# A gated linear recurrence with a gated feed-forward layer: the table that orders all steps is replaced

## The chip, the cores and the metric

The kernel runs on one core of a Trainium2 chip. Five engines work side by side, each through its own queue in order: TensorE (PE; its weight loads are listed as PEld), Vector (DVE), ScalarE (ACT), POOL and SP. SP computes nothing here; it issues DMAs, and so does POOL for the weights and for small accumulating transfers. They wait for each other through semaphores. The metric is the time of one execution in device microseconds; the lower, the better. The measure before is the median of 8 runs.

## The reference

Two parts, the second applied to the output of the first. Batch 4, 8 heads, 768 positions, head width 48; the model width is 8 x 48 = 384, the feed-forward width 1536.

```python
mag = np.sqrt(a_re * a_re + a_im * a_im)
scale = np.minimum(mag, 0.999) / (mag + 1e-06)
a_re_n, a_im_n = (a_re * scale, a_im * scale)
for t in range(S):
    ar, ai = a_re_n[:, :, t, :, None], a_im_n[:, :, t, :, None]
    new_re = ar * S_re - ai * S_im
    new_im = ar * S_im + ai * S_re
    kv = np.einsum('bhd,bhe->bhde', k[:, :, t], v[:, :, t])
    S_re, S_im = (new_re + kv, new_im)
    y[:, :, t] = np.einsum('bhd,bhde->bhe', q[:, :, t], S_re)

x = y.transpose(0, 2, 1, 3).reshape(B * S, H * D)
gate = 1.0 / (1.0 + np.exp(-(x @ w_gate)))
val = x @ w_val
out = gate * val @ w_out
```

The inputs and the output are float32.

## The kernel before

**Slabs and groups.** The 3072 rows are 24 slabs of 128 positions, numbered m = 0 to 23: chunk c of the sequence and batch b give m = 4c + b. SIZES puts the slabs into eight groups of 2, 2, 4, 4, 4, 4, 2 and 2: group 0 holds m = 0 and 1, group 1 m = 2 and 3, group 2 m = 4 to 7.

**Steps.** Every piece of work is a *step* with a kind and a number, written here as kind(number). The kinds that matter, by slab unless said otherwise:

- Loads by SP, 192 KB each (line 556): lr and la (the two parts of a), lk, lq and lv. Stores and small transfers of SP: scr and rbe (decays through DRAM), xk and xq (transposes by DMA, from m = 13), st (output).
- Weights by POOL: wg, wv (line 541) and wo (line 548), three pieces each. Piece i of wg and wv holds the feed-forward blocks 4i to 4i + 3, piece i of wo the same blocks' rows.
- Preparation of a: sq (583 on Vector for m = 2 to 8, else 586 on ScalarE), add (592) and min (599); for a whole group lna, inv and lnm (ScalarE 607, 618, 613), then r for two slabs (624) and atan for the group (702). add, min, r and qke are Vector's in group 0 and POOL's in all others.
- Prefix sums on TensorE: cl (633) of the logarithms and ct (722) of the angles, both in f32 with two instructions each. ee (640, 642) are two exponentials of cl. From chunk 1 on, hop (714, POOL) adds the last row of the chunk before to the angles by an accumulating DMA ahead of ct.
- r16 (728, Vector) rounds the turns, nid (735, TensorE) subtracts them, cr (745, ScalarE) keeps the last row for hop, ab (756, Vector) and cs (767 to 770, ScalarE) give cosine and sine.
- qke (695) multiplies q and k by the exponentials, ks and qs (780, Vector) by cosine and sine. v16 (688, POOL) casts v.
- tp (818, 819) transposes q and k on TensorE and qkT (825, Vector) copies them out, in two halves for each slab up to m = 12. sc (837, TensorE) are the scores of half the heads, mst (845, Vector) masks them.
- u and x16 (859, 868, POOL), kv (877, TensorE) and P (887, 890, Vector) carry the state from chunk to chunk. y (903, 905, TensorE) is the recurrence's output, y16 (522, Vector) its copy, xp (923, TensorE) transposes it, xt (929, Vector) copies it out as input of the feed-forward part.
- Feed-forward, for group g and block fb of 128 columns out of 12: pg(g,fb) and pv(g,fb) (942, TensorE, three matmuls each), tanh(g,fb) (952, ScalarE), p(g,fb) (958, Vector). For each slab, po(m,i) (978, TensorE) in three parts of four blocks, ot (522, Vector) and st.

**What sets the order.** The table TIMES holds one number for every step, and the program emits all steps sorted by it. Each engine's queue is this sorted list cut down to that engine. The numbers are sort keys: what counts is which is larger, and they cause no waiting. The waits come from data and buffers alone.

```python
order = sorted(self.steps, key=lambda k: (at[k], self.rank[k]))
...
for _ in range(WARM.get(key, 0)):
    nc.tensor.matmul(warm_of(tiles[st[2][0]]), zero, zero, start=True, stop=True)
st[0](tiles)
```

**Buffers.** The table SLOTS says which slot of a ring each new tile takes, in the order of the steps: two slots for a (group 2 takes the one of group 0, which ct(0) and ct(1) read last), five for q and k, three for v, four PSUM banks called gen (cl, ct, tp, sc, kv, y, xp) and four called moe (pg, pv, po). A step that takes a slot waits until its former holder's last reader is done.

**Dummies.** WARM puts matmuls of zeros, 128 x 128 (line 1012), in front of a step on TensorE. They write into the tile that the step is about to take, so they too wait until its slot is free.

**Tables of ScalarE.** lna and lnm need one function table, inv and ee one of two, atan one of two, tanh one of three, cs one of two. Where the sorted order goes from one kind to another that the loaded table doesn't hold, a table load is emitted (line 1006).

**The order at the start.** SP's loads are lr(0) la(1) lr(1) la(0) lr(2) la(2) lr(3) lk(1) la(3) lk(2) lv(4) lk(0) lq(1) lq(0) lv(1), and then, from the 16th on, lr(4) la(4) la(5) lr(7) lr(5) lk(3) lq(3) lq(2) lv(0) la(7) la(6) lr(6). lr(4) is the first into the slot that ct(0) and ct(1) free. POOL's steps are add(2) add(3) v16(4) min(2) **wg(1)** r(2) v16(1) add(4) **wv(1)** qke(3) add(5) qke(2) **wg(2)** min(4) v16(0) **wg(0)** add(7) add(6) **wv(2)** min(6) r(6) **wv(0)** r(4), the hops 4 to 7, qke(7) qke(4) **wo(1)** qke(5) add(8) v16(3) **wo(0)** v16(2) add(10) qke(6) **wo(2)**.

Of the kernel before, what the change touches and what calls it, by code (L numbers as in the profile page):

```python
# [36 lines left out]
        32.951, 14.583, 29.638],  # L37
    "wv": [
        41.185, 24.111, 37.481],
    "wo": [  # L40
        56.204, 51.226, 63.509],
    "lr": [
        0.04, 0.86, 3.16, 5.08, 13.925, 19.752, 28.021, 17.531, 29.623,
        62.128, 43.583, 64.048, 57.026, 74.047, 73.257, 65.008, 96.257,
        107.615, 110.045, 101.515, 137.663, 151.768, 166.927, 171.067],
    "la": [
        2.2, 0.45, 4.12, 7, 14.68, 15.64, 25.512, 24.552, 30.593, 69.119,
        51.877, 58.495, 61.138, 75.967, 72.847, 63.088, 97.077, 105.695,
        103.265, 102.675, 139.203, 141.828, 168.878, 168.468],
    "sq": [  # L50
        5.69, 4.73, 9.161, 10.49, 21.424, 23.242, 34.706, 33.84, 44.15,
        72.689, 57.636, 69.729, 66.044, 80.249, 76.577, 70.689, 104.472,
        112.973, 118.73, 115.322, 149.228, 158.967, 174.676, 175.97],
    "add": [
        6.559, 7.025, 10.178, 12.149, 22.441, 26.922, 36.527, 34.857, 53.807,
        73.594, 58.541, 70.634, 66.949, 89.758, 79.981, 72.602, 111.571,
        123.103, 119.884, 117.287, 150.133, 161.218, 175.581, 177.193],
    "min": [
        7.605, 13.68, 30.458, 38.521, 74.873, 71.699, 91.293, 87.116, 124.638,
        121.415, 162.282, 179.123],  # L60
    "lna": [
        6.558, 13.727, 35.687, 78.872, 83.739, 120.761, 160.998, 178.729],
    "lnm": [
        8.185, 15.332, 39.488, 82.363, 93.681, 125.605, 163.249, 180.206],
    "inv": [
        7.426, 14.595, 37.195, 80.986, 91.565, 126.982, 163.986, 180.943],
    "r": [
        8.295, 15.623, 42.005, 39.424, 82.531, 84.291, 93.956, 106.636,
        133.282, 137.885, 164.891, 181.848],
    "cl": [  # L70
        9.073, 9.719, 20.075, 17.308, 43.684, 45.402, 46.048, 42.48, 85.5,
        91.202, 87.197, 87.843, 109.442, 108.149, 111.386, 107.503, 148.529,
        150.473, 145.491, 154.559, 177.162, 179.303, 182.338, 182.984],
    "ee": [
        12.987, 12.247, 22.019, 22.759, 47.25, 48.311, 49.051, 46.51, 90.085,
        92.941, 89.345, 90.825, 111.417, 110.677, 112.233, 109.46, 152.06,
        151.32, 152.8, 155.406, 179.466, 188.022, 187.282, 188.762],
    "scr": [
        30.033, 30.313, 28.711, 28.431, 49.147, 48.867, 50.638, 56.303,
        91.661, 94.511, 90.731, 91.381, 115.548, 116.608, 114.858, 110.455,  # L80
        156.012, 152.178, 156.292, 156.982, 183.077, 198.269, 192.333, 192.613],
    "rbe": [
        47.412, 67.694, 70.599, 98.417, 129.307, 159.322, 213.64, 204.94],
    "lk": [
        9.88, 6.04, 7.96, 20.712, 35.106, 41.425, 53.205, 32.273, 78.847,
        81.727, 83.647, 77.887, 115.138, 96.667, 104.225, 133.664, 114.448,
        116.198, 156.572, 141.418, 176.447, 181.157, 169.288, 172.027],
    "lq": [
        11.8, 10.84, 22.632, 21.672, 38.894, 46.157, 55.893, 37.894, 79.807,
        92.351, 91.941, 82.687, 120.194, 101.105, 109.085, 134.074, 119.784,  # L90
        117.158, 157.262, 146.226, 177.407, 184.327, 178.947, 183.367],
    "lv": [
        23.592, 12.76, 50.228, 49.427, 8.92, 75.007, 80.767, 76.927, 92.761,
        84.607, 114.038, 111.965, 119.374, 136.703, 106.655, 128.527, 145.816,
        94.101, 111.005, 121.814, 191.923, 206.91, 205.76, 172.987],
    "v16": [
        31.509, 17.384, 57.244, 54.761, 13.104, 79.404, 86.539, 81.909,
        103.832, 104.408, 118.728, 120.839, 130.217, 145.197, 110.655,
        132.706, 169.908, 113.392, 127.88, 168.466, 198.411, 218.557, 220.232,
        183.609],  # L100
    "qke": [
        15.915, 14.389, 27.877, 25.162, 49.465, 52.046, 61.748, 47.704,
        95.717, 97.478, 99.239, 92.196, 128.457, 115.039, 135.043, 141.784,
        155.763, 152.242, 166.705, 157.524, 186.109, 196.651, 188.357, 193.916],
    "atan": [
        10.216, 19.618, 43.84, 86.41, 117.353, 147.043, 184.404, 190.796],
    "ct": [
        11.426, 13.076, 25.634, 21, 49.401, 50.047, 52.307, 54.263, 92.496,
        93.142, 95.408, 90.356, 130.362, 122.671, 135.255, 129.716, 155.205,
        163.471, 166.078, 164.117, 193.531, 197.936, 199.73, 198.917],  # L110
    "r16": [
        12.273, 13.923, 26.481, 25.575, 50.248, 50.894, 55.627, 62.519,
        93.343, 96.075, 99.028, 91.869, 133.139, 123.937, 138.869, 133.605,
        156.052, 164.944, 167.011, 169.332, 195.244, 199.482, 202.877, 203.943],
    "nid": [
        13.722, 14.523, 27.081, 26.727, 50.848, 51.817, 56.538, 64.118,
        95.245, 96.701, 104.303, 94.435, 135.093, 128.568, 141.444, 137.196,
        156.948, 165.748, 170.162, 171.619, 196.323, 200.376, 205.919, 214.499],
    "cr": [
        19.248, 20.355, 30.395, 30.765, 55.525, 55.895, 58.653, 66.781,  # L120
        97.782, 101.447, 107.796, 98.152, 137.227, 144.056, 144.426, 141.165,
        158.597, 170.192, 185.618, 173.352],
    "ab": [
        18.25, 15.449, 28.61, 27.546, 52.95, 52.484, 59.067, 64.782, 95.609],
    "cs": [
        18.25, 17.363, 28.61, 29.608, 52.95, 54.738, 59.067, 64.782, 100.183,
        99.026, 106.162, 103.315, 135.456, 129.652, 141.807, 139.532, 157.44,
        166.112, 170.562, 172.195, 196.687, 201.864, 206.282, 214.862],
    "ks": [
        19.692, 18.716, 29.74, 32.974, 54.147, 56.093, 63.916, 66.125,  # L130
        102.751, 101.019, 108.206, 110.129, 136.745, 130.941, 143.096,
        148.631, 159.249, 167.943, 175.372, 184.196, 200.213, 210.119,
        207.571, 216.165],
    "qs": [
        22.29, 20.558, 31.205, 37.37, 57.07, 59.923, 69.298, 68.432, 104.816,
        101.885, 109.263, 110.995, 140.302, 131.807, 145.477, 149.497,
        164.078, 170.962, 176.838, 185.062, 202.011, 215.299, 208.437, 222.773],
    "tp": [
        28.731, 23.29, 26.28, 21.645, 35.6, 35.154, 40.597, 38.934, 62.039,
        59.39, 67.868, 65.458, 81.249, 79.852, 77.107, 78.532, 112.679,  # L140
        117.708, 115.091, 104.466, 123.54, 114.644, 118.804, 116.388, 153.513,
        146.785],
# [139 lines left out]
}  # L282
SLOTS = {
    "a2": "01010101",
    "sq": "011010101010101010111010",
    "qk": "043210342031430124134023",
    "lm": "01010101",
    "v32": "021021021020102201212012",
# [754 lines left out]
```

## Time and profile before

| | us |
|---|---|
| median of 8 runs | 266.51 |
| lowest and highest run | 264.64 and 269.81 |
| the profiled execution, its own time | 266.67 |
| its span, first to last instruction | 264.9 |

| engine | busy us | share of the span | instructions |
|---|---|---|---|
| PE | 250.9 | 95% | 2445 |
| PEld | 173.3 | 65% | 2445 |
| DVE | 210.8 | 80% | 373 |
| ACT | 182.5 | 69% | 304 |
| POOL | 160.5 | 61% | 170 |

The page of the profile lists lines and engines with their busy time; "idle before" names what an engine waited for last. The windows cut the span into stretches and give the busy time of every engine in each. The chain of waits is followed back from the last instruction, at each step to what released it. TensorE's matmuls overlap in the record: one of 128 columns is recorded with 219 ns, while the next starts 56 ns later. So the distance from start to start is what a row of matmuls costs, not the recorded duration. PE's busy time includes the dummies, 465 in all.

### The profile page before, as it was taken

The numbers are of one execution on the slowest core, as the hardware profiler recorded it, in microseconds if no ns is written. First come the engines' busy times: TensorE is split into PE (matmuls) and PEld (weight loads), VectorE is DVE, ScalarE is ACT, GpSimd is POOL, SyncE is SP. The second block draws the span as 40 slices with busy tenths as digits, with TensorE's granted clock in tenths as the row PEclk, the third lists the DMA queues.
The fourth block names the chain that finished last, engine by engine and source line by source line (L and its number), as shares of the span: only waits on it lengthen the run. The fifth ranks groups of instructions, "written<-read, shape, count | busy, mean of one in ns | idle before, by whom it ended". The sixth has DMA issues, their size and how long they took to land.

```text
span 264.9 us, 6444 instructions
## 1 busy us (share of the span) xinstructions
PE 250.9 (95%) x2445; PEld 173.3 (65%) x2445; DVE 210.8 (80%) x373; ACT 182.5 (69%) x304; POOL 160.5 (61%) x170
## 2 busy tenths in 40 slices
PE   8598987799999999999999999999999999999995
PEld 8377786568788864557774456754557644678784
DVE  2749799369989964999989888988668978986552
ACT  2988358677377999999585897889993674114150
POOL 1182959799159999659998969881879400420000
PEclk9899999999999999999999999999999999999999
DMA  6989999979979928899939997589985278641001
GB/s 135 207 149 201 185 197 176 190 118 196 196 68 206 206 68 175 126 204 192 179 77 168 191 172 137 83 198 181 201 163 73 89 139 153 62 119 63 30 32 59
DMA packets 175022, 38.18 MB, mean 144 GB/s; under 512 B 167928, under 2 KB 174992, under 8 KB 174992
## 3 DMA queue, kind: packets, MB, share of 16 engines
q1 hardware_dynamic: 170368, 34.20, 68.4%
q0 software_dynamic: 4624, 3.57, 9.3%
q8 instruction: 19, 0.31, 0.5%
q14 instruction: 11, 0.09, 0.1%
HBM read 30.74 MB, written 4.76 MB: 134 GB/s over the span
## 4 chain that ended last, share of the span: by engine, by line
PE 67%; DMA 11%; POOL 7%; SPq 4%; issue 4%; DVE 3%; ACT 2%; POOLq 0%; ACTq 0%; DVEq 0%
PE o L978 16%; PE g L942 14%; PE v L942 14%; PE ct L722 6%; PE cl L633 4%; SPq L556 3%; PE sc L837 3%; DMA wv<-in_moe_w_val_dram 3%; DMA qk<-in_k_dram 2%; DMA rbe<-scr 2%; POOL qk L695 2%; DMA qk<-in_q_dram 2%; PE y L905 2%; DMA a<-in_a_re_dram 1%; PE y L903 1%
## 5 line engine op out<-in xcount | busy, mean ns | idle before, releaser
L952 ACT ACTIVATE g<-g 128x256 f16<-128x256 f32 (+1 forms) x96 | 44.6, 492 | 37.8 <-PE g L942 29.6
L958 DVE SCALAR_TENSOR_TENSOR p<-g,v 128x256 f16<-128x256 f16 (+1 forms) x96 | 50.7, 549 | 14.7 <-PE v L942 7.5
L942 PE MATMUL v<-xt,wv 128*128 128x256 f16 (+1 forms) x288 | 58.4, 326 | 1.3 <-DMA wv<-in_moe_w_val_dram 0.7
L942 PE MATMUL g<-xt,wg 128*128 128x256 f16 (+1 forms) x288 | 57.9, 325 | 0.4 <-DVE p L958 0.3
L978 PE MATMUL o<-wo,p 128*128 128x384 f16 (+1 forms) x300 | 55.6, 319 | 0.0
L592 POOL TENSOR_TENSOR lm<-sq 128x384 f32<-128x384 f32 x22 | 27.1, 1232 | 33.2 <-DVE sq L583 18.2
L695 POOL TENSOR_TENSOR qk<-qk,ee 128x768 f32<-128x768 f32 x22 | 43.6, 2055 | 0.6 <-DMA qk<-in_q_dram 0.3
L942 PEld LDWEIGHTS <-wv 128*128 128x128 f16 x288 | 27.3, 98 | 20.9 <-issue 2.7
L942 PEld LDWEIGHTS <-wg 128*128 128x128 f16 x288 | 27.4, 97 | 19.5 <-issue 3.2
L845 DVE TENSOR_TENSOR mst<-sc,msk_t 128x512 f16<-128x512 f32 x48 | 31.8, 683 | 8.5 <-PE sc L837 8.0
L978 PEld LDWEIGHTS <-p 128*128 128x128 f16 x300 | 27.1, 98 | 13.0 <-issue 0.2
L1006 ACT ACT_TABLE_LOAD x27 | 34.6, 1283 | 0.5
L1012 PEld LDWEIGHTS <-zero 128*128 128x128 f16 x465 | 30.0, 103 | 6.9 <-issue 5.2
L780 DVE TENSOR_TENSOR kst<-qk,cs 128x768 f16<-128x768 f32 x24 | 25.1, 1046 | 2.4 <-issue 1.2
L780 DVE TENSOR_TENSOR qst<-qk,cs 128x768 f16<-128x768 f32 x24 | 23.8, 995 | 0.0
L633 PE MATMUL cl<-lm,wl_t 128*128 128x384 f32 x48 | 20.1, 519 | 3.6 <-ACT lm L613 2.9
L624 POOL TENSOR_TENSOR a<-a 128x768 f32<-128x768 f32 x11 | 19.9, 1815 | 3.1 <-ACT a L618 2.7
L714 POOL DMA_DIRECT2D a<-cr x20 | 16.9, 1028 | 5.9 <-ACT a L702 5.6
L722 PE MATMUL ct<-a,wt_t 128*128 128x384 f32 x48 | 19.6, 503 | 0.5 <-DMA v<-in_v_dram 0.4
L768 ACT ACTIVATE cs<-ct 128x384 f32<-128x384 f32 x24 | 11.8, 491 | 10.6 <-DVE cs L756 10.6
L688 POOL TENSOR_SCALAR v<-v 128x384 f16<-128x384 f32 x24 | 15.4, 642 | 5.8 <-DMA v<-in_v_dram 3.2
L728 DVE TENSOR_SCALAR r<-ct 128x384 f16<-128x384 f32 x24 | 13.1, 551 | 6.8 <-PE ct L722 6.8
(71 smaller groups left out, 446.1 us busy)
## 6 DMA issues: line engine op xcount, KB each, us to landing
a<-in_a_re_dram SPq DMA_DIRECT2D x24, 192.0 KB
a<-in_a_im_dram SPq DMA_DIRECT2D x24, 192.0 KB
qk<-in_k_dram SPq DMA_DIRECT2D x24, 192.0 KB
v<-in_v_dram SPq DMA_DIRECT2D x24, 192.0 KB
qk<-in_q_dram SPq DMA_DIRECT2D x24, 192.0 KB
out_dram<-ot SPq DMA_DIRECT2D x23, 192.0 KB
wg<-in_moe_w_gate_dram POOLq DMA_DIRECT2D x3, 384.0 KB, 5.3
wv<-in_moe_w_val_dram POOLq DMA_DIRECT2D x3, 384.0 KB, 6.6
```

The costliest lines, as they stand in the source:

```text
L592: eng(g).tensor_tensor(out=T[LM][:, s], in0=T[SQ][:, 0], in1=T[SQ][:, 1], op=ALU.add)
L633: nc.tensor.matmul(T[CL][:, :HD], wl_t, T[LM][:, s], start=True, stop=True)
L695: eng(g).tensor_tensor(out=T[QK], in0=T[QK], in1=T[EE], op=ALU.mult)
L722: nc.tensor.matmul(T[CT][:, :HD], wt_t, T[A][:, 1, s], start=True, stop=False, skip_group_check=True)
L780: nc.vector.tensor_tensor(out=T[SL][i].rearrange("p h (r x) -> p h r x", r=2)[:, :, :, 0:D], in0=heads(T[QK][:, i]).unsqueeze(2) .broadcas ...
L845: nc.vector.tensor_tensor(out=T[MS], in0=T[SC], in1=msk_t.unsqueeze(1).broadcast_to([L, 4, L]), op=ALU.mult)
L942: nc.tensor.matmul(T[ACC][:, :nt], w[:, j, fb * 128:fb * 128 + 128], T[XT][:, j, :nt], start=(j == 0), stop=(j == 2))
L952: nc.scalar.activation(out=T[G16][:, :nt], in_=T[PG][:, :nt], func=FT.Tanh, scale=0.5)
L958: nc.vector.scalar_tensor_tensor(out=T[PT][:, fb, :nt], in0=T[G16][:, :nt], scalar=1.0, op0=ALU.add, in1=T[PV][:, :nt], op1=ALU.mult)
L978: nc.tensor.matmul(T[PO][:, :wd], T[PT][:, fb, s * L:(s + 1) * L], wo16[:, fb, c0:c0 + wd], start=(fb == 0), stop=(fb == NFB - 1))
L1006: nc.scalar.preload_act_table_set(SETS[key[1]])
L1012: nc.tensor.matmul(warm_of(tiles[st[2][0]]), zero, zero, start=True, stop=True)
```

## The change

No step is added or removed, and no step does other work. Three tables are new: TIMES (all rows), SLOTS and WARM. The code that reads them is the same.

```diff
 TIMES = {
     "wg": [
-        32.951, 14.583, 29.638],
+        37.918, 12.723, 48.717],
     "wv": [
-        41.185, 24.111, 37.481],
+        41.621, 25.156, 30.759],
     "wo": [
-        56.204, 51.226, 63.509],
+        55.774, 58.421, 64.847],
...
 WARM = {
-    ('cl', 0): 86,
-    ('ct', 0): 19,
-    ('ct', 1): 18,
-    ('sc', 0, 0): 62,
-    ('sc', 0, 1): 4,
-    ('sc', 1, 0): 15,
-    ('sc', 1, 1): 18,
-    ('y', 1): 12,
-    ('pg', 0, 1): 3,
-    ('pg', 0, 3): 18,
-    ('pv', 0, 4): 13,
-    ('pg', 0, 7): 5,
-    ('pv', 0, 7): 8,
-    ('pg', 0, 10): 15,
-    ('cl', 2): 38,
-    ('cl', 3): 47,
-    ('ct', 2): 34,
-    ('ct', 3): 5,
-    ('y', 3): 12,
-    ('cl', 4): 6,
-    ('cl', 7): 23,
-    ('sc', 6, 0): 4,
+    ('cl', 0): 65,
+    ('ct', 0): 29,
+    ('sc', 0, 0): 61,
+    ('sc', 0, 1): 3,
+    ('sc', 1, 0): 12,
+    ('sc', 1, 1): 22,
+    ('pv', 0, 2): 6,
+    ('pg', 0, 4): 2,
+    ('pv', 0, 4): 9,
+    ('pg', 0, 6): 8,
+    ('pv', 0, 6): 4,
+    ('pv', 0, 7): 9,
+    ('cl', 3): 42,
+    ('ct', 2): 42,
+    ('ct', 3): 4,
+    ('sc', 3, 0): 16,
+    ('pg', 1, 0): 3,
+    ('pg', 1, 11): 4,
+    ('cl', 5): 2,
+    ('sc', 6, 1): 3,
+    ('pg', 2, 4): 2,
 }
```

What the new keys make of the queues, as far as the prediction speaks of it:

- Dummies: 348 instead of 465; ahead of pg(1,0), the first gate matmul of group 1, 336 instead of 461.
- POOL begins v16(4) add(2) **wg(1)** add(3) min(2) r(2) v16(1) add(4) **wv(1)** add(5) qke(2) qke(3) **wv(2)** add(6) add(7) min(4) **wg(0)** min(6) r(6) **wv(0)** v16(0) r(4) v16(3), the hops 5, 4, 6, 7, **wg(2)** qke(7) qke(5) add(8) qke(4) **wo(0)** v16(2) **wo(1)** qke(6) **wo(2)**. One piece of wg stays first of the weights, all three of wv now come ahead of the last one of wg.
- SP's loads begin lr(0) la(1) la(0) lr(1) lr(2) la(2) lv(4) lr(3) lk(1) la(3) lk(0) lk(3) lq(1) lv(1) lq(0), then lr(4) lr(5) la(4) lq(3) lk(2) la(5) lq(2) lr(7) la(7), scr(2), lr(6) la(6) lk(7) lv(0) lk(4) lk(5) lq(5) lr(8) la(8), scr(0), lv(3).
- ScalarE begins sq(0) sq(1) lna(0) lnm(0) inv(0), so that lnm(0) stands ahead of inv(0) (before lna, inv, lnm); 29 table loads are emitted between its steps instead of 27.
- Vector: r(0) ahead of sq(2) and sq(3); qs(2) sq(6) sq(7) mst(0,1) mst(0,0) ks(3), where before it was ks(2) qkT(0,0) qs(2) mst(0,1) ks(3) sq(7) sq(6). Later ks(4) qs(4) p(0,5) ab(6) ks(5) instead of ks(4) r16(6) ks(5) qs(4); sc and mst of the second halves of m = 2 and 3 come behind xt(0) and xt(1).
- TensorE: pg(0,6) is the first feed-forward step and comes ahead of cl(5), cl(6) and cl(4); before it was pv(0,0), behind all four cl of group 2. The same set of steps stands ahead of pg(1,0) in both orders.
- Stages after that: the same steps in another order on every engine.

## The prediction

> **What bounds the kernel now.** First the windows, cut where the second group's feed-forward begins (busy us and count of PE, PEld, DVE, ACT, POOL, then TensorE's clock, DMA share, GB/s), and the same for line 1012, the dummies, alone; then the chain of waits from 36 to 76 us; then the timelines of DVE, POOL and PE in that stretch; last SP's waits and DMA by queue.
>
> ```profile
> span 264.9 us, 6444 instructions
> ...
> 0.00:75.00 75.00, 64.84 (x788) 53.19 (x789) 56.02 (x100) 49.39 (x78) 45.60 (x48) 0.98 1.00 175
> 75.00:265.00 190.00, 186.08 (x1660) 120.11 (x1657) 154.76 (x274) 133.10 (x226) 114.86 (x122) 1.00 0.70 132
> ...
> 0.00:75.00 75.00, 31.60 (x461) 29.68 (x461) 0.98 1.00 175
> 75.00:265.00 190.00, 0.39 (x4) 0.27 (x4) 1.00 0.70 132
> ```
>
> After 75 us TensorE is busy 186.1 of 190 us, with 4 dummies. There it is the bound, and the work is the same in both kernels. Before 75 us 31.6 of its 64.8 busy us are dummies. So the end moves with one moment: when pg(1,0), the first gate matmul of group 1, can start.
>
> ```profile
> 74.08 0.62 DVE L929 COPY xt<-xp 128x384 f16<-128x384 f16 x2
> ...
> 74.76 0.49 PE L942 MATMUL g<-xt,wg 128*128 128x256 f16 x3
> ...
> 59.46 1.33 DVE L780 TENSOR_TENSOR kst<-qk,cs 128x768 f16<-128x768 f32 x1 [0.22 <-issue]
> ...
> 39.01 2.60 POOL L592 TENSOR_TENSOR lm<-sq 128x384 f32<-128x384 f32 x2 [2.62 <-DVE sq L583]
> ...
> 45.95 1.82 POOL L624 TENSOR_TENSOR a<-a 128x768 f32<-128x768 f32 x1
> 49.59 3.24 POOL L714 DMA_DIRECT2D a<-cr  x4 [1.82 <-ACT a L702]
> 51.72 4.71 POOL L695 TENSOR_TENSOR qk<-qk,ee 128x768 f32<-128x768 f32 x2
> ```
>
> Vector's copy xt(3) ends at 74.70 and the matmul follows 0.06 us later. From ks(4) at 59.46 to that copy, 15.25 us, Vector's timeline has only about 0.4 us of gaps: Vector sets this stage. ks(4) itself comes from group 2's preparation, which runs through POOL: two adds from 39.01, the products r, the arctangent, four hops from 49.59, then the qke products.
>
> ```profile
> 45.10 6.63 DMA wv<-in_moe_w_val_dram
> ...
> 53.15 1.00 PE g L1012 x18
> ...
> 62.07 0.82 PE y L1012 x12
> 62.88 0.20 PE y L905 x8
> 63.08 0.84 PE g L1012 x15
> ...
> SPq L556 <- PE ct L722: 5.8, 4, 2.9
> ```
>
> The chain goes through the landing of wv piece 0 and then through dummies; SP stands up to 2.9 us until TensorE releases the first slot of a.
>
> **The work of the change.** No instruction's work changes; the order does, and the dummies.
>
> *Ledger.* From starts of neighbouring matmuls (0.056 us for 128 columns, 0.109 for 256, 0.216 for 512, 0.162 for 384 in f16, 0.323 in f32) all real TensorE work sums to 214 us. Before pg(1,0) stands the same set in both orders, 31.3 us, and behind it 183.0 us. Now: 74.76 + 183.0 + 3.3 (last matmul to end, 261.6 to 264.9) leaves 3.8 us of late stalls and dummies.
>
> *Dummies, 465 to 348.* 117 x 0.056 = 6.6 us of TensorE. Ahead of pg(1,0) they go from 461 to 336, and this I cost at nothing, because Vector's stage covers it; without that cover it would be 125 x 0.056 = 7.0 us gained. Behind that point 4 become 12 (three of them directly ahead of it): 8 x 0.056 = +0.4 us, on a busy TensorE, bounds 0 and 0.4.
>
> *Start.* cl(0) loses 21 dummies: nothing, since TensorE already stands 2.9 us until lm is ready at 10.48. ct(0) gets 29 for 19 and ct(1) none for 18. The four cl matmuls and the next 18 dummies run at about half clock (107 ns a dummy), and the clock is back at 14.5. So ct(0) starts at 14.5 + 11 x 0.056 = 15.2 for 14.60, and ct(1) ends 0.4 to 0.5 earlier. That releases the slot of a, and with it lr(4) and all SP loads behind it: 17.25 becomes 16.8. Transfers were saturated (share 1.00 up to 75 us), so this is worth at most 0.5 us in the loads of group 2.
>
> *Group 2 on Vector.* Now ks(2), qkT, qs(2), one mst, ks(3) come ahead of sq(7), sq(6). After, sq(6) and sq(7) follow qs(2): mst (0.60), ks(3) (0.87) and the copy qkT (0.60) no longer stand ahead. 2.1 us earlier: 37.7 for 39.79, if la(6), now 26th load where lr(6) was 27th, is there. Bounds 0 and 2.1.
>
> *Group 2 on POOL.* From the adds to r(4)'s end it takes 47.77 - 39.01 = 8.76 us now, with two weight issues inside. After: adds 2.60, min 0.82, wg(0) 0.85, min 0.82, r 1.82, wv(0) 0.85, v16(0) 0.51 to 1.10, r 1.82: 10.1 to 10.7. That gives back 1.3 to 1.9 of the 2.1: the arctangent ends 0.2 to 0.8 earlier, at 48.5 to 49.1. Then v16(3) is put ahead of the hops; it is 0.51 to 1.10 long and waits for lv(3), the 34th load. Behind it queue the four hops (for them ct(4) to ct(7)), wg(2) and all qke of group 2. From 2 to 50 us the hardware queue moved 6.70 MB, 34 loads, in 72% of 48 us, 1.0 us each; six weight pieces took 32%, 2.6 us each. 34 x 1.0 + 4.5 x 2.6 + 2 = 48 us with wg(2) out of the way; with all six pieces ahead 52. By the nearest row, the first. Hops at 49.3 for 49.59.
>
> *qke(4).* Now it is the second product behind the hops, after it is fourth behind wg(2), qke(7), qke(5) and add(8). In starts: hops 4 x 0.53, wg 0.82, two qke at 1.77, add 0.95, then 1.8 to 2.9 for itself: 9.2 to 10.4 us behind the first hop, 58.5 to 59.7. cs(4) is then done, so ks(4) starts at about 59.2 for 59.46, -0.3. Wherever it slips, the p products behind it on Vector wait, and with them TensorE's PSUM tiles.
>
> *Vector from ks(4) to xt(3).* The same list as now, except that r16(6) (0.47) is done earlier and p(0,11) (0.34) comes later: -0.8. pg(1,0): 74.76 - 0.3 - 0.8 = 73.7.
>
> *Later stages.* ScalarE gets 29 table loads between steps for 27, 2 x 1.28 us, at nothing: it is 69% busy, and TensorE waited for it after 75 us for only 0.2 us without a break in between. Uncovered +2.6. The 3.6 us of late stalls outside dummies belong to this order; a new one may have none or twice as much, -3.6 to +3.6; I take the same.
>
> *Clock.* At 7.4 to 10.5 us TensorE stood 2.9 us, and the windows show 0.50 to 0.56 from 11 to 14 us; from 14.5 it is 1.00 despite shorter gaps. After, 125 fewer dummies leave new gaps, the longest between sc(0,1) and sc(1,1), whose dummies take the PSUM slot that mst(0,1) frees, on Vector behind sq(7): from about 35.8 to 38.3 by the times above, 2.5 us, an estimate. Priced from the row: 3.4 us at half clock cost TensorE 1.7 us at most, 0 where Vector sets the pace; I take 0. The Trainium skill ("TensorE: Matmul & The Clock Gate", "What's actually happening") states that a free-running window of about 3.4 us without activity halves the clock, which speaks against taking dummies away. By that rule a new gap of 2.5 us alone would not halve it, by the gap of 2.9 us seen here it might; the sum by the harsher reading would be 1.7 us more.
>
> **Sum.** -0.3 - 0.8 + 0.4 = -0.7 us: span 264.2. The profiled execution took 266.67 with span 264.9; it stands 0.16 above the median 266.51. So 266.5 - 0.7 = 265.8 us, no change: within 0.5% (1.3 us), about what a measurement of this kernel can tell.
>
> **Rivals.**
>
> *Faster: the dummies were on the path.* For: the chain view has 18 + 12 + 15 dummies (2.66 us) as its own links from 53 to 64 us, with 8 and 5 smaller ones 58, 3.4 us; after, the stretch from pv(0,0) on holds 30 (1.7 us) where 74 (4.1) stood, and wv(0) is issued about 1 us sooner. Against: Vector without gaps from 59.46. If it holds, 2.4 us more go: 263.4.
>
> *Slower: POOL's new queue.* Place: v16(3) ahead of the hops, then wg(2) and qke(5) ahead of qke(4). Each us that the hops start later moves ks(4), xt(3) and the end by one. With lv(3) landed at 52 and 1.1 us for v16(3) the hops start at 53.1, 3.8 late: 269.6. It decides from hops at about 51.4 on (265.8 + 2.1 = 267.9). For: transfers saturated to 50 us, POOL's hop chain tight. Against: only 4 or 5 pieces ahead of lv(3).
>
> *Slower in the late stages.* Twice the late stalls, or two uncovered table loads: +2.6 to +3.6, 268.4 to 269.4. For: TensorE has no reserve there, and POOL is about 90% busy from 80 to 110 us. Against: its waits after 75 us are a few tenths each.
>
> That the change does nothing is excluded: all engines' orders differ.
>
> **How the numbers follow.** Forecast (265.2 to 267.8 as its own range) 0.36; faster 0.32; POOL's queue 0.17; late stages 0.15. Faster by over 0.5%: 0.32; within: 0.36; slower: 0.32. The range reaches to 262.2, the faster case with a third of the late stalls gone too, and to 269.7, POOL's case.
>
> **What would show it.** In the profile after: about 336 dummies up to pg(1,0) and that step at 73 to 74.5; Vector without gaps from ks(4) to xt(3); sq(7) done by 38; first hop at 49 to 50; qke(4) ended by 60; clock 1.00 from 14.5 on. Wrong, if pg(1,0) starts under 72.5 (dummies), the hops over 51.4 (POOL), or if pg(1,0) is as said and the end is off by over 2 us (late stages).

## The result

| | before | after |
|---|---|---|
| median, us | 266.34 (53 runs) | 268.17 (18 runs) |
| lowest and highest | 264.64 and 269.81 | 267.24 and 271.10 |
| the profiled execution, its time and span | 266.67, 264.9 | 267.98, 266.3 |

The ratio is 1.0088, with a 95% interval from 1.0066 to 1.0110: the change costs 0.9%. The forecast was no change, 265.8 us; the measured value lies inside the range given and next to the rival "slower in the late stages" (268.4 to 269.4). Medians here and below are of all executions; ratios leave out those over 1.5% above the fastest of the same kernel.

### The profile page after: what moved, and what is told of

Its sections match the earlier page's. It is cut to its first block, busy times and chain, and to the rows that moved or that the text cites. A ratio compares the mean times of both kernels' runs of the same rounds, so it can differ in the third digit from the quotient of the medians.

```text
span 266.3 us, 6211 instructions
## 1 busy us (share of the span) xinstructions
PE 244.5 (92%) x2328; PEld 165.5 (62%) x2328; DVE 212.7 (80%) x373; ACT 185.3 (70%) x306; POOL 164.6 (62%) x170
## 4 chain that ended last, share of the span: by engine, by line
PE 40%; POOL 19%; ACT 12%; SPq 9%; DMA 9%; issue 6%; DVE 4%; POOLq 0%; ACTq 0%; DVEq 0%
PE o L977 12%; PE v L941 9%; PE g L941 8%; SPq L555 6%; POOL lm L591 3%; POOL qk L694 3%; POOL a L623 3%; SPq L654 2%; ACT L1005 2%; DMA qk<-in_q_dram 2%; POOL a L713 2%; DMA wo<-in_moe_w_out_dram 2%; PE cl L632 2%; PE sc L836 2%; POOL lm L598 2%
## 5 line engine op out<-in xcount | busy, mean ns | idle before, releaser
L951 ACT ACTIVATE g<-g 128x256 f16<-128x256 f32 (+1 forms) x96 | 45.3, 495 | 42.1 <-PE g L941 23.4
L941 PE MATMUL v<-xt,wv 128*128 128x256 f16 (+1 forms) x288 | 60.6, 326 | 1.8 <-ACT g L951 1.3
L977 PE MATMUL o<-wo,p 128*128 128x384 f16 (+1 forms) x300 | 55.0, 319 | 0.4 <-DMA wo<-in_moe_w_out_dram 0.4
L977 PEld LDWEIGHTS <-p 128*128 128x128 f16 x300 | 27.1, 97 | 14.5 <-issue 1.0
L779 DVE TENSOR_TENSOR kst<-qk,cs 128x768 f16<-128x768 f32 x24 | 26.4, 1103 | 5.2 <-POOL qk L694 3.3
L1011 PEld LDWEIGHTS <-zero 128*128 128x128 f16 x348 | 22.5, 103 | 7.2 <-issue 4.0
L687 POOL TENSOR_SCALAR v<-v 128x384 f16<-128x384 f32 x24 | 16.2, 673 | 10.8 <-DMA v<-in_v_dram 8.9
L632 PE MATMUL cl<-lm,wl_t 128*128 128x384 f32 x48 | 19.3, 505 | 3.6 <-ACT lm L612 3.2
L623 POOL TENSOR_TENSOR a<-a 128x768 f32<-128x768 f32 x11 | 20.5, 1875 | 3.0 <-ACT a L617 2.5
L824 DVE COPY qkT<-tp 128x1024 f16<-128x1024 f16 x26 | 17.5, 683 | 0.9 <-PE tp L818 0.7
L585 ACT ACTIVATE sq<-a 128x768 f32<-128x768 f32 x17 | 13.9, 841 | 5.7 <-DMA a<-in_a_im_dram 4.3
```

The lines of the kernel that those rows point to most:

```text
L623: eng(g).tensor_tensor(out=T[A][:, 1, i:j], in0=T[A][:, 1, i:j], in1=T[A][:, 0, i:j], op=ALU.mult)
L632: nc.tensor.matmul(T[CL][:, :HD], wl_t, T[LM][:, s], start=True, stop=True)
L779: nc.vector.tensor_tensor(out=T[SL][i].rearrange("p h (r x) -> p h r x", r=2)[:, :, :, 0:D], in0=heads(T[QK][:, i]).unsqueeze(2) .broadcas ...
L941: nc.tensor.matmul(T[ACC][:, :nt], w[:, j, fb * 128:fb * 128 + 128], T[XT][:, j, :nt], start=(j == 0), stop=(j == 2))
L951: nc.scalar.activation(out=T[G16][:, :nt], in_=T[PG][:, :nt], func=FT.Tanh, scale=0.5)
L977: nc.tensor.matmul(T[PO][:, :wd], T[PT][:, fb, s * L:(s + 1) * L], wo16[:, fb, c0:c0 + wd], start=(fb == 0), stop=(fb == NFB - 1))
```

## The profile after

First the page's first line and the windows, cut where those of before were cut: busy time and count of PE, PEld, DVE, ACT and POOL, TensorE's clock, DMA share, GB/s; then the same for line 1011, the dummies, alone.

```profile
span 266.3 us, 6211 instructions
...
0.00:75.00 75.00, 58.79 (x683) 46.84 (x684) 55.75 (x101) 51.73 (x82) 47.19 (x50) 1.00 0.99 177
75.00:265.00 190.00, 185.66 (x1645) 118.68 (x1644) 156.95 (x273) 133.53 (x225) 117.44 (x121) 1.00 0.69 131
...
0.00:75.00 75.00, 23.66 (x339) 21.75 (x339) 1.00 0.99 177
75.00:265.00 190.00, 1.00 (x9) 0.71 (x9) 1.00 0.69 131
```

Behind 75 us TensorE looks as full as before, 185.7 for 186.1 of 190 us. From this view nobody would find the loss. The timelines of the steps that the prediction followed (start us, us, engine, line, operation, out<-in, count, and in brackets the idle time before and what ended it):

```profile
36.11 2.60 POOL L591 TENSOR_TENSOR lm<-sq 128x384 f32<-128x384 f32 x2 [2.77 <-DVE sq L582]
...
45.31 1.81 POOL L623 TENSOR_TENSOR a<-a 128x768 f32<-128x768 f32 x1
47.52 0.79 POOL L687 TENSOR_SCALAR v<-v 128x384 f16<-128x384 f32 x1 [0.40 <-DMA v<-in_v_dram]
48.94 3.29 POOL L713 DMA_DIRECT2D a<-cr  x4 [0.64 <-ACT a L701]
...
56.42 2.96 POOL L694 TENSOR_TENSOR qk<-qk,ee 128x768 f32<-128x768 f32 x1
...
59.41 0.96 DVE L779 TENSOR_TENSOR kst<-qk,cs 128x768 f16<-128x768 f32 x1 [1.39 <-POOL qk L694]
...
71.36 0.61 DVE L928 COPY xt<-xp 128x384 f16<-128x384 f16 x2
...
73.00 0.82 PE L941 MATMUL g<-xt,wg 128*128 128x256 f16 x6
```

pg(1,0) starts at 73.00 for 74.76: the first 75 us went better than forecast (73.7). So 1.76 us were won there, and the end came 1.4 us later all the same. Much of the 1.76 is the clock: TensorE runs at half clock from 11.1 to 14.5 us in the profiled execution of the kernel before, and nowhere behind 4.8 us in this one. The profile of old_with_one_more_table (below), whose order is that of the kernel before up to 94 us, has no half clock behind 5.0 us and starts pg(1,0) at 73.71. So at equal clock the new head wins about 0.7 us in these two executions. In the other profiles with the new head and no added dummies pg(1,0) starts between 72.52 and 74.33.

**Where the lead went.** The busy share can't show it: a matmul is recorded longer than the distance to the next start (0.219 for 0.056 us at 128 columns), so a short wait between two matmuls still counts as busy. This sum can: the time at which TensorE starts a step, less the real work (no dummies) that stands ahead of it by the start-to-start prices of the prediction. It is the time lost so far. Each row takes the first step with at least so much real work ahead of it; all values are from the profiled executions.

| real work ahead, us | reached in the kernel before at | lost before | lost after | new_head_old_tail | new_without_late_dummies |
|---|---|---|---|---|---|
| 30 | 73.7 | 43.4 | 41.5 | 41.6 | 41.2 |
| 36 | 79.6 | 43.6 | 42.3 | 43.2 | 41.5 |
| 54 | 99.4 | 44.9 | 43.6 | 45.1 | 42.7 |
| 66 | 111.4 | 45.3 | 44.9 | 45.5 | 44.0 |
| 72 | 117.9 | 45.3 | 45.3 | 45.5 | 44.4 |
| 108 | 154.8 | 46.2 | 46.2 | 46.0 | 45.3 |
| 162 | 209.4 | 47.2 | 47.3 | 47.3 | 46.4 |
| 168 | 215.7 | 47.2 | 48.3 | 47.3 | 47.4 |
| 210 | 257.5 | 47.4 | 48.7 | 47.4 | 47.7 |

(The last two columns are experiments, below.) In the kernel after, the lead of 1.9 us is gone at 118 us; then both kernels lose the same until about 209 us; there the kernel after loses 1.0 us more within 6 us. The two places in its timelines, ScalarE and TensorE at 101 to 111 us, and POOL, Vector and TensorE at 206 to 213 us:

```profile
101.79 1.28 ACT L1005 ACT_TABLE_LOAD   x1
103.34 1.49 ACT L612 ACTIVATE lm<-lm 128x1536 f32<-128x1536 f32 x1 [0.26 <-POOL lm L598]
104.84 1.28 ACT L1005 ACT_TABLE_LOAD   x1
...
110.37 0.81 PE L941 MATMUL v<-xt,wv 128*128 128x512 f16 x3 [0.67 <-ACT g L951]
...
206.75 2.62 POOL L694 TENSOR_TENSOR qk<-qk,ee 128x768 f32<-128x768 f32 x1
...
207.96 2.24 DVE L779 TENSOR_TENSOR kst<-qk,cs 128x768 f16<-128x768 f32 x1
210.12 0.54 DVE L727 TENSOR_SCALAR r<-ct 128x384 f16<-128x384 f32 x1
...
210.72 0.32 PE L734 MATMUL ct<-r,nid_t 128*128 128x384 f16 x1 [0.23 <-DVE r L727]
```

At the first, lnm(4) (103.34) stands between two sets of tanh and so needs a table of its own; with the one at 94.75 us these are three loads where the kernel before has two, and TensorE then waits 0.67 us for a tanh, 0.83 us by the sum above. At the second, a ks that takes 0.96 us elsewhere takes 2.24 beside a qke on POOL; behind it on Vector stand r16 and two ot, on which TensorE waits three times (0.39, 0.30 and 0.32 us from start to start, beyond the price of the step ahead).

**A lead given back, or an order that loses?** If only the lead were given back, a kernel with the new order behind pg(1,0) but a late pg(1,0) would lose nothing at these two places. The same sum for all 14 profiled executions (the experiments are below) shows that it does:

| order behind pg(1,0) | profiled executions | pg(1,0) starts at, us | lost from 54 to 72 us of work | from 162 to 168 us |
|---|---|---|---|---|
| of the kernel before | before, old_without_ff_dummies, old_with_first_dummies, old_pg_delayed, new_head_old_tail, new_head_tanh_before_sq12 | 74.1 to 76.9 | 0.42 to 0.44 | 0.00 |
| the same, one table load more | old_with_one_more_table | 73.7 | 2.66 | 0.00 |
| of the kernel after | after, new_without_late_dummies, new_v16_behind_hops, new_more_early_dummies, old_head_new_tail | 72.5 to 79.6 | 1.33 to 1.71 | 0.95 to 1.00 |
| the same, ks(20) later | new_ks20_later, new_ks20_more_dummies | 73.7 and 74.1 | 2.12 and 1.64 | 0.00 |

In new_v16_behind_hops pg(1,0) starts at 74.33, and TensorE waits for the same tanh as long as in the kernel after:

```profile
110.90 0.81 PE L941 MATMUL v<-xt,wv 128*128 128x512 f16 x3 [0.67 <-ACT g L951]
```

So the new order loses some 2 us at these two places whether pg(1,0) comes early or late. From pg(1,0) to the last matmul the kernel before loses 3.9 us and the kernel after 7.0; new_v16_behind_hops and new_more_early_dummies, with the same order there and a later pg(1,0), lose 6.0. Of the 3.1 us that the kernel after loses more, about 2.1 are thus its order's own, and about 1.0 is lead given back.

The page's chain of waits has turned too. By engine it was PE 67%, DMA 11%, POOL 7%, ACT 2%; after:

```profile
PE 40%; POOL 19%; ACT 12%; SPq 9%; DMA 9%; issue 6%; DVE 4%; POOLq 0%; ACTq 0%; DVEq 0%
```

TensorE is no longer what the end hangs on for 60% of the span.

## The experiments

Ratios are to the kernel before on the same chip, with 95% intervals. Where an order is built from two, the keys are numbered anew and the slots follow from them.

### Whose fault: the new head or the new tail

**new_head_old_tail.** The order, slots and dummies of the kernel after for all steps that stand ahead of pg(1,0) there, and all other steps in the order of the kernel before. 340 dummies, 27 table loads.

```diff
 order of the keys in TIMES
   ahead of ('pg', 1, 0): as in the kernel after
-  from ('pg', 1, 0) on: as in the kernel after
+  from ('pg', 1, 0) on: as in the kernel before
```

> All steps up to pg(1,0) in the new order, all others in the old one. Theory L (the new order wins some 1.8 us up to pg(1,0) and its own order behind that point loses 3.2): pg(1,0) at about 73.0, and then 186.6 us as in the kernel before to the last matmul, end 1.3 to 1.8 us under the kernel before, 264.5 to 265.0. Rival G (whatever is won early is given back, because Vector, POOL or the loads set the end in the late stages): 266.0 to 266.5, the same as before, with pg(1,0) early and more stalls behind it.

Measured: 267.49 us, ratio 1.0052 [1.0026, 1.0078]. The lead is lost here too, and sooner: the table shows it gone at 54 us of work. From there on this run loses what the kernel before loses. What stopped it stands at the seam of the two orders. On TensorE, tp(5) is ahead of pg(1,0) only in the kernel before and tp(7) only in the kernel after, the first half of each (the two sets of steps are equal in size, not the same); here both are ahead, TensorE waits 0.65 us for a copy P on Vector before tp(5), and pg(1,0) starts at 74.14. Then two rows of ScalarE's timeline:

```profile
74.70 0.84 ACT L544 ACTIVATE sq<-a 128x768 f32<-128x768 f32 x1 [1.91 <-DMA a<-in_a_im_dram]
75.45 0.64 ACT L910 ACTIVATE g<-g 128x256 f16<-128x256 f32 x2
```

sq(12) stands in ScalarE's queue ahead of tanh(1,0) and waits 1.91 us for its load. In the kernel before it had run at 72.58, when nobody waited for it. So this run shows what the mixed order does with a lead. It doesn't show that the old order can't use one: in old_with_one_more_table, whose pg(1,0) starts 1.05 us earlier than in the kernel before, that lead still stands at 54 us of work.

**old_head_new_tail.** The reverse.

```diff
 order of the keys in TIMES
   ahead of ('pg', 1, 0): as in the kernel before
-  from ('pg', 1, 0) on: as in the kernel before
+  from ('pg', 1, 0) on: as in the kernel after
```

> All steps up to pg(1,0) in the old order, all others in the new one. Theory L: pg(1,0) at 74.8 and then 189.8 us as in the changed kernel, 3 us over the kernel before, 269 to 270. Rival G: the end is set by the late order alone, 268.2 as the changed kernel, or, if no order matters there, 266.3.

Measured: 273.02 us, ratio 1.0260 [1.0236, 1.0284], worse than either. Some 5 us go at the seam, where ScalarE stands 3.2 us ahead of two sq and TensorE then 2.1 us for a tanh; the windows there (columns as above):

```profile
76.75:80.16 3.41, 1.30 (x11) 0.93 (x10) 0.28 (x1) 2.62 (x5) 2.23 (x3) 1.00 0.98 93
80.16:83.57 3.41, 3.41 (x16) 1.97 (x15) 1.59 (x4) 0.38 (x1) 1.38 (x2) 0.50 1.09 213
```

TensorE is busy 1.30 of 3.41 us, and the clock is 0.50 in the next 3.41 us. This run says that head and tail belong together; what the new tail costs by itself its time doesn't say. Behind the seam it loses at the two places what the kernel after loses (second table).

### Dummies

**old_without_ff_dummies.** The kernel before without the 74 dummies from pv(0,0) on, the question of the rival "faster".

```diff
-    ('pg', 0, 1): 3,
-    ('pg', 0, 3): 18,
-    ('pv', 0, 4): 13,
-    ('pg', 0, 7): 5,
-    ('pv', 0, 7): 8,
-    ('y', 3): 12,
-    ('pg', 0, 10): 15,
```

> The kernel before without its 74 dummies in the first feed-forward stretch. Theory V (Vector sets that stretch and covers the dummies, as the prediction said): 0 to -0.5 us, 265.8 to 266.4, pg(1,0) at 74.3 to 74.8. Rival D (the dummies that the chain of waits lists are on the path): -2.4 to -4.1 us, 262.2 to 263.9.

Measured: 266.74 us, ratio 1.0023 [0.9999, 1.0048]; pg(1,0) came 0.4 us earlier in the profile, at 74.36. 4.1 us of dummies left and no gain shows: the 2.4 us that the rival "faster" saw in the links of the chain of waits are not there. A gain of some tenths could be hidden, since these executions have more stretches at half clock (1.25 each, for 0.60 in the kernel before on this chip; see "The clock").

**new_without_late_dummies.** The kernel after without the 12 dummies from pg(1,0) on.

```diff
-    ('pg', 1, 0): 3,
-    ('pg', 1, 11): 4,
-    ('sc', 6, 1): 3,
-    ('pg', 2, 4): 2,
```

> The changed kernel without its 12 dummies from pg(1,0) on. Theory L with the late loss in waits: 12 x 0.056 = 0.7 us at most, three of them covered, so 267.5 to 268.1. If the dummies hold TensorE where a release would come anyway: no change, 268.2.

Measured: 267.55 us, ratio 1.0062 [1.0041, 1.0082], 0.26% or 0.7 us below the kernel after; the two intervals overlap, so the gain is not clear of noise. Twelve dummies are 0.67 us at 0.056. In the table this kernel keeps a lead of 0.8 to 0.9 us from 72 to 162 us of work, and loses it in the place at 209 us.

### Does the end move with pg(1,0)?

**old_pg_delayed.** One line in the kernel before.

```diff
 WARM = {
+    ('pg', 1, 0): 32,
```

> The kernel before with 32 dummies ahead of pg(1,0), 1.8 us of TensorE. Theory T, the end moves with pg(1,0) as the prediction took it: 1.8 us longer, 268.0. Theory S, other engines set the stage behind it: TensorE catches up and the time is 0.2 to 0.9 us longer. Neither expects a gain.

Measured: 268.18 us, ratio 1.0071 [1.0042, 1.0099], 1.8 us more by the medians: the whole delay reaches the end, as the premise of the prediction has it. TensorE's timeline:

```profile
75.16 1.95 PE L1013 MATMUL g<-zero 128*128 128x128 f16 x32
76.94 0.82 PE L943 MATMUL g<-xt,wg 128*128 128x256 f16 x6
```

So with the old order behind it a later pg(1,0) moves the end. For an earlier one the executions of the kernel before itself say something. Some have a stretch of 3.41 us at half clock, some none ("The clock" says how that is told). In 91 of them, on five chips, the 42 with one took 1.04 us more than the 49 without (standard error 0.12, with a level of its own for each chip), and in the profiles pg(1,0) starts at 74.76 with that stretch and, in old_with_one_more_table, at 73.71 without it. So in the old order an early pg(1,0) goes with an early end; that it makes it is not shown.

**new_head_tanh_before_sq12.** new_head_old_tail with the queue mended: sq(12) with its add behind tanh(1,5), and tp(5,0) behind pg(1,5).

```diff
 "sq":  m = 12
-    31.8
+    32.75
 "add": m = 12
-    31.9
+    32.76
 "tp":  m = 5, first half
-    32.1
+    32.35
```

> The new order up to pg(1,0) and the old one behind it, as in new_head_old_tail, with three keys changed: sq(12) on ScalarE, which there stood 1.9 us in front of tanh(1,0) until its load had landed, goes behind tanh(1,0) and tanh(1,5) (and add(12) with it), and tp(5,0) goes behind pg(1,5). Theory Q, the lead of 1.8 us at pg(1,0) was lost to that one queue: pg(1,0) at 72.9 to 73.2, the lead is still 1.2 to 1.8 us when ScalarE loads the table for lna(3) (82.5 to 83.0 for 84.08), from there the old order keeps it, and the time is 1.0 to 1.8 us below the kernel before, 264.4 to 265.4. Theory S, another engine or the loads hold this stage back anyway: the lead is under 0.5 us at 100 us, and the time is within 0.5 us of the 267.5 of new_head_old_tail.

Measured: 267.87 us, ratio 1.0057 [1.0019, 1.0095], no better than new_head_old_tail. So mending this one queue is not enough. The profiled execution is a poor test of the rest: TensorE runs at half clock from 38.5 to 48.7 us in it, and pg(1,0) starts only at 74.24. In it the wait moved on to the next load, as ScalarE's and SP's timelines show:

```profile
74.77 0.71 ACT L910 ACTIVATE g<-g 128x256 f16<-128x256 f32 x2 [0.61 <-PE g L900]
...
85.49 0.84 ACT L544 ACTIVATE sq<-a 128x768 f32<-128x768 f32 x1 [2.12 <-DMA a<-in_a_re_dram]
...
73.40 5.89 SPq L613 DMA_DIRECT2D rbe<-scr  x6
79.33 0.70 SPq L514 DMA_DIRECT2D a<-in_a_im_dram  x1
```

tanh(1,0) now follows pg(1,0) directly, but sq(14) waits 2.12 us for la(14) and lr(14), and these stand in SP's queue behind the rbe transfers, which take SP from 73.40 to 79.29, six in a row. This is the seam again: in the kernel before SP issues two at 71.86 and two at 75.20, with a load between them. ScalarE's closed block of table load, lna(3), inv, lnm begins at 86.62 us, for 84.08 in the kernel before. (This profiled execution was 1.4 us above the median of its kernel, so its size is not typical; whether its order of waits is, no second profile shows.)

**old_with_one_more_table.** One key of the kernel before: tanh(2,8) ahead of lnm(4).

```diff
 "tanh": (2, 8)
-    96.829
+    93.5
```

> The kernel before with one key changed: tanh(2,8) goes ahead of lnm(4) on ScalarE, so that this engine loads three tables where it loaded two between 94 and 103 us (28 in all for 27), as the new order does there. Theory A, ScalarE has no reserve from 84 to 116 us, so that TensorE waits for it: 1.28 us more at 110 us, of which 0.8 to 1.3 are left at the end, 267.0 to 267.6. Theory C, as the prediction took it, the load is covered: within 0.3 us of the kernel before.

Measured: 270.42 us, ratio 1.0129 [1.0075, 1.0184], by the ratio 3.4 us (2.0 to 4.9) more, more than either theory. ScalarE and TensorE:

```profile
99.39 0.67 ACT L952 ACTIVATE g<-g 128x512 f16<-128x512 f32 x1
100.08 1.28 ACT L1006 ACT_TABLE_LOAD   x1
101.37 1.48 ACT L613 ACTIVATE lm<-lm 128x1536 f32<-128x1536 f32 x1
102.87 1.28 ACT L1006 ACT_TABLE_LOAD   x1
104.17 1.09 ACT L952 ACTIVATE g<-g 128x512 f16<-128x512 f32 x2
...
104.81 0.81 PE L942 MATMUL v<-xt,wv 128*128 128x512 f16 x3 [2.00 <-ACT g L952]
```

The load of 1.28 us, with the tanh in front of it, becomes a wait of 2.00 us on TensorE. This is the term that the prediction set at nothing. The kernel before has 0.2 us of such waits behind 75 us. The profiled execution is the fastest of the six: it loses 2.66 us from 54 to 72 us of work for 0.44, and 1.1 of these 2.2 us are left in its span, as its pg(1,0) came 1.05 us earlier. Why the other executions are longer still no profile shows.

### The place at 209 us

**new_ks20_later.** new_without_late_dummies, with ot(14) ahead of qs(20) on Vector and ks(20) behind it.

```diff
 "ks": m = 20
-    199.487
+    201.2
 "ot": m = 14
-    202.357
+    201.1
```

> The kernel after without the 12 late dummies, as in new_without_late_dummies, with two keys changed: on Vector ot(14) goes ahead of qs(20) and ks(20) behind it, so that r16(22) and the two copies ot that release PSUM no longer stand behind a ks of 2.2 us, and ks(20) no longer runs beside POOL's qke of 2.6 us. Theory V, the three stalls of TensorE at 210 to 212 us (0.38, 0.30 and 0.32 us) come from that place on Vector: they go, ks(20) takes about 1.0 us, and the time falls by 0.7 to 1.0 us, to 266.6 to 266.9, 0.2 to 0.4% above the kernel before. Rival W, the time is given to a later wait for ks(20) and qs(20): no more than 0.3 us below new_without_late_dummies.

Measured: 267.08 us, ratio 1.0032 [1.0003, 1.0062], 0.30% or 0.8 us by the ratios below the kernel that it was made from; their intervals overlap. Vector's timeline:

```profile
209.47 0.56 DVE L723 TENSOR_SCALAR r<-ct 128x384 f16<-128x384 f32 x1 [0.34 <-PE ct L717]
209.95 1.01 DVE L517 TENSOR_SCALAR ot<-o 128x384 f32<-128x384 f32 x2
210.88 0.99 DVE L775 TENSOR_TENSOR kst<-qk,cs 128x768 f16<-128x768 f32 x1
```

ks(20) takes 0.99 us for 2.24, and none of the three stalls is left between 209 and 213 us: the time lost from 162 to 168 us of work is 0.00 for 1.00, in new_ks20_more_dummies too. What this place costs TensorE is shown; that the time fell by as much is likely, no more.

### The clock

The mean granted clock of an execution tells how often TensorE ran at half clock: one stretch of 3.41 us in a span of 265 lowers it by 0.0064. In 49 executions of the kernel before there are 0 or 1 such stretches (mean 0.55), in 57 of five kernels with the new head 0 to 4 (mean 2.1). Within these 57, with a level of its own for each kernel, each stretch goes with 0.48 us more (standard error 0.10). The profiled execution of the kernel after has none, so its profile says nothing of this. But the low clock isn't what makes the kernel after slower in the main: its three executions without such a stretch took 267.25 to 267.98 us, while of the 49 of the kernel before without one the median is 265.50 and one alone is above 267.25. In new_head_old_tail it may be: the four executions with at most one stretch took 266.0 to 266.7 us, as the kernel before, and the five with more 267.5 to 269.0. Three experiments put dummies back.

**old_with_first_dummies.**

```diff
-    ('cl', 0): 86,
+    ('cl', 0): 120,
```

> The kernel before with 120 dummies ahead of cl(0) for 86, which reach into the gap of 3.1 us that TensorE has there, from 7.3 to 10.5 us, ahead of the half clock at 11.1 to 14.5. Theory K: that stretch at half clock, present in 27 of 49 executions of the kernel before, goes in nearly all, and the median falls by 0.4 to 0.6 us, to 265.6 to 266.0: a version that beats both. Rival L: within 0.2 us of the kernel before.

Measured: 265.65 us beside 265.49 for the kernel before on the same chip, ratio 1.0006 [0.9982, 1.0030]. All 12 executions have a clock of 0.998 to 1.000, the half clock is gone, and the time stays. Either the 34 dummies cost about what they win, or the half clock marks the longer executions without making them so; the run doesn't tell which.

**new_more_early_dummies** and **new_ks20_more_dummies**, the same edit in the kernel after and in new_ks20_later:

```diff
-    ('cl', 0): 65,
+    ('cl', 0): 105,
-    ('sc', 0, 1): 3,
+    ('sc', 0, 1): 18,
-    ('sc', 1, 1): 22,
+    ('sc', 1, 1): 30,
+    ('y', 1): 14,
+    ('y', 0): 6,
-    ('sc', 3, 0): 16,
+    ('sc', 3, 0): 22,
```

> The kernel after with 89 dummies more in the first 47 us, where its TensorE stands: cl(0) 105 for 65, sc(0,1) 18 for 3, sc(1,1) 30 for 22, y(1) 14 and y(0) 6 for none, sc(3,0) 22 for 16. The order is the same. Theory K, the dummies taken out let the clock drop: in 57 executions with the new head the mean granted clock tells of 2.1 stretches of 3.4 us at half clock, and each goes with about 0.5 us more. Then the mean number falls under 1 and the median by 0.4 to 1.0 us, to 267.2 to 267.8. Rival L, the low clock only marks executions that are late for another reason, or the dummies themselves stand in the way (in old_with_first_dummies the half clock went and the time stayed): within 0.3 us of 268.2 or longer.

> The same 89 early dummies in new_ks20_later (the new order without its 12 late dummies and with ks(20) later). Theory K: 0.4 to 1.0 us below the 267.1 of that kernel, 266.1 to 266.7. Rival L: within 0.3 us of 267.1 or longer.

Measured: 271.31 us, ratio 1.0164 [1.0116, 1.0212], and 268.51 us, ratio 1.0069 [1.0040, 1.0098]: 0.8% and 0.4% slower than without these dummies (the intervals of the second pair overlap). The stretches at half clock fell from 1.9 to 0.8 and from 2.3 to 1.2 per execution, on a chip on which the kernel before had 0.2. So the dummies likely hold the clock up, and they stand in the way by more than it is worth: in both profiles sq(6) on Vector starts 1.0 us later than in the kernel after (36.1 and 36.0 for 35.06). Low clock and long time go together; that the one makes the other is not shown.

**new_v16_behind_hops.** In the profile of new_more_early_dummies, an execution 2.2 us above the median of its kernel, POOL's timeline has these rows:

```profile
51.97 0.51 POOL L689 TENSOR_SCALAR v<-v 128x384 f16<-128x384 f32 x1 [3.43 <-DMA v<-in_v_dram]
52.54 3.29 POOL L715 DMA_DIRECT2D a<-cr  x4
```

v16(3) waits 3.43 us for lv(3), and the hops start at 52.54: the rival "POOL's new queue" at its place and near its moment (it had hops at 53.1 for a load that lands at 52). In the kernel after this wait was 0.40 us. Does it decide there in other executions? One key:

```diff
 "v16": m = 3
-    44.779
+    48.2
```

> The kernel after with one key changed: on POOL v16(3) goes behind the four hops, so that these no longer stand behind a step that waits for the load lv(3). In the profiled execution of the kernel after that wait was 0.40 us, in new_more_early_dummies, where lv(3) was issued 4.5 us later, it was 3.43 us and the time 3 us longer. Theory H, the rival of POOL's queue decides in some executions of the kernel after: those above 269.5 us (5 of 18) go, and the median falls by 0.3 to 0.8 us, to 267.4 to 267.9. Rival N, the loads are in time in all executions: the median within 0.3 us of 268.2, and the same share above 269.5.

Measured: 268.19 us (6 runs), ratio 1.0107 [1.0071, 1.0143], with one of the six at 270.26. No gain shows: in the kernel after this place in POOL's order was not what cost it.

## Why the prediction was wrong, point by point

**The early stages: right in kind, most sizes near.** sq(7) was done at 36.9 (37.7 predicted), the arctangent at 48.6 (48.5 to 49.1), the hops began at 48.9 (49.3), qke(4) ended at 59.4 (58.5 to 59.7) and ks(4) began at 59.4 (59.2). Adds to r(4)'s end took 11.0 us (10.1 to 10.7). ct(0) came at 12.9 for 15.2, since the clock of this execution was 1.00 from 4.8 us on; this clock is part of the early pg(1,0), as said above.

**Vector from ks(4) to xt(3): sign right, size wrong.** Predicted -0.8, measured from 15.25 to 12.56 us, -2.7. "The same list as now" overlooked ks(6) and P(0), which stand behind xt(3) now (P(1) came in), and counted ks(4) and qs(5) at 1.33 and their share of 1.75, where they took 0.96 and 0.95 this time. Vector then was done 1.0 us before pg(1,0): TensorE's own queue, kv(0) and three dummies, ended last.

**The dummies ahead of pg(1,0): right as far as tested.** Without 74 of them the ratio is 1.0023 [0.9999, 1.0048], and "faster" falls. The 12 late ones (+0.4 in the sum, for 8 more) may cost their 0.67 us; 0.26% is measured, not clear of noise.

**The step that failed: the late stalls, "I take the same", and with them the table loads "at nothing".** The sum left 3.8 us of stalls and dummies behind pg(1,0) in both kernels. Measured as time lost from pg(1,0) to the last matmul it is 3.9 us before and 7.0 us after. The bounds that the prediction gave this term (-3.6 to +3.6) hold it; its middle was carried over from the old order. Two places make 2.3 us of the difference. From 54 to 72 us of work the kernel after loses 1.71 for 0.44: ScalarE's block has three table loads for two there. One load more in that block, put into the kernel before, makes it 2.66 for 0.44, and the time 3.4 us longer by the ratio, not 0. In the kernel after the extra load stands at the same place with another order around it; of the 0.83 us that TensorE then waits at 110 us it is the likely part, but it couldn't be taken away alone there, since lnm(4) would then wait for POOL's min. From 162 to 168 us it loses 1.00 for 0.00, where ks(20) stands beside a qke; moved behind it, 0.00. Both belong to the rival "slower in the late stages"; the mechanism of the second, Vector beside POOL, was not among those foreseen.

**The step that failed with it: "So the end moves with one moment".** It was read off 186.1 busy us of 190, with "the work is the same in both kernels". The work is, the order is not, and the order sets what is lost behind that moment. With the order left alone a delay reaches the end in full (old_pg_delayed). With the new one about 1.0 us of the lead is given back as well, a part of it where a po waits 0.38 us for a late piece of wo. What feeds TensorE had little slack in that stretch: in the kernel before ScalarE is busy 9.9 of 10 us from 90 to 100 us.

**Account in the profiled executions.** A lead of 1.9 us just ahead of pg(1,0); back to 0 at 118 us (0.6 by 80 us, with that po; 0.9 from 105 to 111 us, with ScalarE's tanh late; 0.4 by 118 us); -0.1 to 209 us; -1.0 from there to 216 us; -0.3 behind it: 1.4 us late at the last step, as the spans say. Of the signs that the prediction named for its own failure, this is the third: pg(1,0) about as said and the end over 2 us off (268.17 for 265.8).

**What stays open.** In the medians less is shown than in the profiles. Without the late dummies and the stalls at 209 us 0.56% of the 0.88% are gone (1.0032 [1.0003, 1.0062] for 1.0088 [1.0066, 1.0110]); the two steps of this, 0.26% and 0.30%, are not clear of noise one by one. 0.32% [0.03, 0.62] is left in new_ks20_later. It holds ScalarE's block and whatever the low clock costs, and no run here splits the two. No order tried here is faster than the kernel before.

## What to carry over

When a change replaces the order of every stage, the stalls behind the bottleneck are a term to be worked out for the new order, not to be carried over: a busy share of 98% hid 3.9 us in one order and 7.0 in the other. To tell a lead given back from an order that loses, compare the time lost stage by stage in executions that reach the stage early and late. A chain of waits that ends in dummies or fillers need not be a price; leave them out once and see. And price a table load by the stretch it falls into: ScalarE was idle for 30% of the span, but in the stretch in question it was busy 9.9 of 10 us, and one load of 1.28 us became a wait of 2.00 us.

## What was not expected of the hardware

**TensorE's clock falls behind a thin stretch, not only behind an empty one.** The prediction weighed a rule of the Trainium skill ("TensorE: Matmul & The Clock Gate", "What's actually happening"): a free-running window of about 3.4 us decides. The windows agree, 3.41 us long and with another phase in every execution. The page speaks of an idle window. These rows, first from new_head_tanh_before_sq12 and then from the kernel after, show windows that are not idle:

```profile
35.06:38.47 3.41, 1.38 (x26) 1.26 (x24) 3.41 (x6) 1.49 (x2) 2.33 (x2) 1.00 1.16 189
38.47:41.88 3.41, 2.62 (x26) 2.27 (x23) 2.36 (x3) 1.96 (x2) 3.18 (x4) 0.50 0.74 144
```

```profile
35.55:38.96 3.41, 1.42 (x26) 1.42 (x26) 3.41 (x5) 2.01 (x2) 2.76 (x3) 1.00 1.18 196
38.96:42.38 3.42, 2.17 (x32) 1.70 (x29) 3.25 (x5) 1.82 (x3) 3.20 (x4) 1.00 0.79 157
```

With 1.38 us of 3.41 busy the next window is at 0.50, with 1.42 it is at 1.00; the 1.30 us in old_head_new_tail fit. Recorded busy time is not the measure, though. In old_without_ff_dummies 1.78 us are followed by half clock:

```profile
58.88:62.30 3.42, 1.78 (x26) 1.22 (x24) 3.42 (x5) 2.29 (x5) 3.27 (x3) 1.00 1.23 205
62.30:65.71 3.41, 3.04 (x19) 2.38 (x19) 3.19 (x6) 1.78 (x5) 3.25 (x4) 0.50 0.99 138
```

Counted by the start-to-start prices (and 0.025 us for 48 columns), with the windows laid from each execution's own changes of clock, one limit fits all 14 profiles. Of the windows at full clock, the 22 with TensorE at work for at most 0.380 of the window are followed by half clock, and the 1026 with 0.388 or more by full clock. With the phase differing between executions, one program can fall on either side; that this alone gives the 0 to 4 stretches is likely, but no program here was profiled twice.

**A Vector instruction waits out POOL's.** ks(20) took 2.24 us beside a qke of 2.62, and 0.99 where it was moved behind it; it ended 0.83 us after that qke. In the kernel before the ks at 107.99 (1.72 us) and the qs at 65.28 (1.75 us) end 0.82 us after the qke beside them. The Trainium skill ("SBUF — State Buffer", "Who interferes with whom") says that a Vector instruction with two inputs in SBUF, as ks is, contends with a POOL instruction that reads SBUF, and calls the port that they share an exclusive lock. The rows agree: what is left of ks(20) once the qke ends is nearly its full length.
